# Cosine attention and leaky-ReLU MLP on one core: a written list of operations up to the third batch's second unit

## The chip, the cores and the metric

One core of a Trainium2 chip. The metric is device time in microseconds (us) of one execution. Engines are called as in the profile: PE is TensorE (PEld its weight loads), DVE VectorE, ACT ScalarE, POOL GpSimd, SP SyncE, which here only issues DMAs.

## The reference

```python
q_n = q / (norm(q) + 1e-06);  k_n = k / (norm(k) + 1e-06)
scores = q_n @ k_n^T / tau                       # tau = 0.1
attn = exp(scores - max);  attn = attn / (sum + 1e-09)
x = (attn @ v), heads side by side               # [3584, 768]
h = x @ w_in;  g = maximum(0.01 * h, h)          # w_in [768, 2048]
out = g @ w_out                                  # w_out [2048, 768]
```

8 batches, 12 heads, 448 positions, head size 64. Inputs are float32; the matmuls run in bf16.

## The kernel before, in words

**Slots.** The work on q and k is cut into 48 slots. In batches 0 and 1 a slot `s` is a pair of heads with q and k (slots 0 to 11, `OLD` = 12). From then on two slots make a unit: one holds q, the other k, of two pairs of heads. A slot goes through these steps:

- `load_qk` (L144): DMAs on SP into one of four `qk_h` buffers. Slots 0 to 5 come by `load_main` and `load_rem` (L129, L138) into `xT` memory.
- `squares` (L211): multiplies on POOL, for old slots in two parts (0 is q with the 64 remainder positions of q and k, 1 is the main part of k); slots 0 and 1 on ACT.
- `sums` (L228): reduce on DVE. `roots` (L244): Ln and Exp on ACT, which give the norms. `normalise` (L252): a small reduce, a reciprocal and one or two multiplies on DVE, which give `qn` in bf16.
- Old slots: `transposes` (L300), seven PE transposes into a PSUM bank and a DVE copy to `qkT`. New ones: a DVE transpose into `tt`, and after the unit's second slot six DMAs on SP from `tt` to `qkT`.

**Attention.** Old slots: `scores` (L334) makes a tile of scores of 128 keys for two heads (tile 3 holds the remainder keys of two slots), in two PSUM banks, and an ACT exp (L357) to a `pe` tile follows. For two slots together (`j`), `totals` (L375) adds up the exps on PE and takes Ln and inverse on ACT; `products` (L385) multiplies by v on PE, once for each parity `e` of the head size; `scale` (L394) writes to `xT` on DVE. New units: `quad_tiles` (L408) with exps at L425, then `group_products` (L429), `group_logs`, `group_inverse`, `group_scale`.

**MLP.** The tokens go in 8 chunks `c` of 384 and 512 columns in turn. `first(c, m)` (L487) is six matmuls against `w_in` and a Prelu on ACT into `hT`; with fewer `kts` it does part of the six, and the bank is kept. `second(c, ts, half)` (L525) is 16 matmuls against `w_out`, a DVE copy to `osb`, and an SP DMA to `out` when a row of results is full.

**Order.** `manual_schedule` (L48): each engine takes its instructions in the order in which the program names them, and semaphores hold what depends on another engine. For the first two batches the order is a loop over slots 0 to 5 (L654 to L736) and then a list of calls (L747 to L863). From there on a planner makes visits of three score tiles (L868 to L962): it deals the MLP's groups to visits by their cost, and gives each visit the steps of one slot.

**PSUM.** `banks` (L75) deals the eight banks: the one dealt longest ago. While `deals["apart"]` holds, which is until L747, pairs come out of banks 0 to 3 and single ones out of 4 to 7. An instruction that writes a bank waits until the earlier content has been read.

**Fills and holds.** `fill(n)` (L604) issues `n` matmuls on ones that nobody reads: 20 at the start (L611), 17 more among the first slots. `hold` (L617) is a copy of one element of `qn` on POOL: POOL's next work waits for that slot's `normalise`. It stands ahead of nearly all `squares`. `hold_loads` (L614) is an SP DMA of one element of `qn`: the next `load_qk` waits for it. It stands ahead of the loads of slots 8, 9, 12, 13 and 14.

**POOL's DMAs.** v (`load_v` L173, `load_v_rem` L180, `load_vq` L196), `w_in` in four pieces (L102) and `w_out` in three (L108) are issued on POOL, between the squares.

Of the kernel before, what the change touches and what calls it, by code (L numbers as in the profile page):

```python
# [12 lines left out]
AX = mybir.AxisListType  # L13


@with_exitstack
def kernel(
# [25 lines left out]
    WARM = 20  # L43
    NEWQ = 2 * NQ
    PER = 3
# [25 lines left out]
    age = [0] * 8  # L71
    kept = {}
    deals = {"n": 0, "apart": True, "width": 128}

    def banks(count, keep=None):  # L75
        lo, hi = (0, 8) if not deals["apart"] else (0, 4) if count == 2 else (4, 8)
        x = min(
            (i for i in range(lo, hi, count) if not set(range(i, i + count)) & set(kept.values())),
            key=lambda i: max(age[i : i + count]),
        )  # L80
        deals["n"] += 1
        age[x : x + count] = [deals["n"]] * count
        if keep:
            kept[keep] = x
        return ps[:, x] if count == 1 else ps[:, x : x + count]

    def given_back(keep):
        deals["n"] += 1
        age[kept.pop(keep)] = deals["n"]

# [115 lines left out]
    def squares(s, eng=gp, parts=(0, 1)):  # L211
        if s >= NSLOT:
            return
        sq = sqt[s % 3]
        if s >= OLD:
            sqs[s] = sq
            x = raw[s].rearrange("p (t d) -> p t d", d=D)
            gp.tensor_tensor(sq[:, :, :D], x, x, op=ALU.mult)  # L218
            return
        sqs[s] = halves(sq.rearrange("p t d -> p (t d)"), D + 1)  # L220
        for i in parts:
            x, y = raw[s][i], sqs[s][i]
            if eng is nc.scalar:
                nc.scalar.activation(y[..., :D], x, func=AF.Square)
            else:
                eng.tensor_tensor(y[..., :D], x, x, op=ALU.mult)  # L226

    def sums(s, parts=(0, 1)):  # L228
        if s >= NSLOT:
            return  # L230
        if s not in ss:
            ss[s] = smp.tile([128, 14], F32, name="ss")
        if s >= OLD:
            nc.vector.tensor_reduce(  # L234
                ss[s], sqs[s], axis=AX.X, op=ALU.add
            )
            return
        for i in parts:
            o = ss[s][:, 0:8] if i == 0 else ss[s][:, 8:14]
            nc.vector.tensor_reduce(  # L240
                o.rearrange("p (h t) -> p h t", h=2), sqs[s][i], axis=AX.X, op=ALU.add
            )

    def roots(s):  # L244
        if s >= NSLOT:
            return
        nc.scalar.activation(ss[s], ss[s], func=AF.Ln)  # L247
        nc.scalar.activation(norms[s % 3][:, :, 0], ss[s], func=AF.Exp, scale=0.5)  # L248
# [3 lines left out]
    def normalise(s):  # L252
        if s >= NSLOT:
            return
# [29 lines left out]
    def one(tp, s, lo, hi):  # L284
# [10 lines left out]
    def transposed():  # L295
        return banks(1).bitcast(BF16)[:, : 7 * 128].rearrange("p (t c) -> p t c", c=128)
# [3 lines left out]
    def transposes(s):  # L300
        if s >= NSLOT:
            return
        if s >= OLD:
            u, which = divmod(s - OLD, 2)
            if which == 0:
                turned[u] = ttp.tile([128, 2, 2, S], BF16, name="tt")
            to = turned[u][:, :, which].bitcast(F32)
            nc.vector.transpose(  # L308
                out=to.rearrange(("p g (c m) -> p m g c", "p g (m c) -> p m g c")[which], m=7),
                in_=qn[s].bitcast(F32).rearrange("p m (g c) e -> p m g (c e)", g=2),  # L310
            )
            if which == 0:
                return
            for w, pair in enumerate(UNITS[u][1]):
                dst = qtp.tile([128, 2, S], BF16, name="qkT")
                for r0, of, n, g in ((0, 0, 32, 0), (32, 0, 64, 1), (96, 32, 32, 0)):
                    nc.sync.dma_start(
                        out=dst[r0 : r0 + n],
                        in_=turned[u][64 * w + of : 64 * w + of + n, g],
                    )  # L320
                qkT[pair] = dst.rearrange("p t c -> p (t c)")
            return
        dst = qtp.tile([128, 7, 128], BF16, name="qkT")
        qkT[s] = dst.rearrange("p t c -> p (t c)")
        tp = transposed()
        one(tp, s, 0, 7)
        nc.vector.tensor_copy(out=dst, in_=tp)
# [6 lines left out]
    def scores(s, kis):  # L334
        key_tiles([(s, ki) for ki in kis])

    def key_tiles(which):

        tiles = []
        for s, ki in which:  # L340
            sc = banks(2)
            tiles.append(sc)
            width = deals["width"] if ki < 3 else min(deals["width"], 64)
            for p in range(0, 128, width):
                x, c0 = (qkT[s - 1 + p // 64], 448 + p % 64) if ki == 3 else (qkT[s], 512 + 128 * ki + p)
                for a in range(2):
                    rows = slice(64 * a, 64 * a + 64)
                    nc.tensor.matmul(  # L348
                        out=sc[p : p + width, a, :S], lhsT=x[rows, c0 : c0 + width],
                        rhs=x[rows, 0:S], start=True, stop=True,  # L350
                    )
        for (s, ki), sc in zip(which, tiles):
            if ki == 3:
                dst = pr[s // 2] = pe_tile()
            else:
                dst = pe[s, ki] = pe_tile()
            nc.scalar.activation(out=dst, in_=sc[:, :, :S], func=AF.Exp, scale=inv_tau)  # L357
# [17 lines left out]
    def totals(j):  # L375
        sm = banks(1)
        strip_products(j, sm, lambda g, ki: ones, lambda g: ones_rem[:, g // 2])
        rb = rbp.tile([128, 2, S], F32, name="rb")[:, 0]
        nc.scalar.activation(rb, sm[:, :S], func=AF.Ln)
        nc.scalar.activation(rb, rb, func=AF.Exp, scale=-1.0)  # L380
        rbs[j] = rb

    pos = {}

    def products(j, e, po=None):  # L385
        b, jj = divmod(j, NQ)
        if po is None:
            po = banks(1, (j, e))
        pos[j, e] = po
        vm = vb[j].rearrange("p h t (d e) -> p h t e d", e=2)  # L390
        vr = vrb[b % 2].rearrange("p j g (d e) -> p j g e d", e=2)
        strip_products(j, po, lambda g, ki: vm[:, g, ki, e], lambda g: vr[:, jj, g, e])

    def scale(j, e):  # L394
        b, jj = divmod(j, NQ)
        m, half = divmod(b, 2)
        if m not in xT:
            xT[m] = xtp.tile([128, KT, 2 * S], BF16, name="xT")
        nc.vector.tensor_tensor(
            xT[m][:, 2 * jj + e, half * S : (half + 1) * S], pos.pop((j, e))[:, :S], rbs[j],  # L400
            op=ALU.mult,
        )
        if (j, e) in kept:
            given_back((j, e))
# [3 lines left out]
    def quad_tiles(which):  # L408

        tiles = []  # L410
        for u, i in which:
            sc = banks(2)
            tiles.append(sc)
            for strip in range(4):
                x = qkT[UNITS[u][1][strip // 2]]
                c0 = S + 64 * i + 32 * (strip % 2)
                for a in range(2):
                    rows = slice(64 * a, 64 * a + 64)
                    nc.tensor.matmul(  # L419
                        out=sc[32 * strip : 32 * strip + 32, a, :S], lhsT=x[rows, c0 : c0 + 32],  # L420
                        rhs=x[rows, 0:S], start=True, stop=True,
                    )
        for (u, i), sc in zip(which, tiles):
            pq[u, i] = pe_tile()
            nc.scalar.activation(out=pq[u, i], in_=sc[:, :, :S], func=AF.Exp, scale=inv_tau)  # L425
# [3 lines left out]
    def group_products(g, e):  # L429


        us = [u for u, (gg, _) in enumerate(UNITS) if gg == g]
        two = len(us) == 2
        po = banks(2)
# [14 lines left out]
        return po  # L449

    def group_logs(g, po):
        grb[g] = rbp.tile([128, 2, S], F32, name="rb")
        nc.scalar.activation(grb[g], po[:, :, :S], func=AF.Ln)
# [10 lines left out]
    def group_scale(g, e, po):  # L464
        js = GROUPS[g]
        for w in range(2):
# [6 lines left out]
            for n in range(2):  # L473
# [4 lines left out]
                )  # L478

# [7 lines left out]
    def first(c, m, kts=range(KT)):  # L487
        c0, n = chunk_cols(c)
        if c not in hT:
            hT[c] = htp.tile([128, MT, 512], BF16, name="hT")  # L490
        if (c, m) in begun:
            pm, done = begun.pop((c, m))
        else:
            pm, done = banks(1, (c, m, "begun") if len(kts) < KT else None), 0
# [7 lines left out]
        if done + len(kts) < KT:  # L502
            begun[c, m] = pm, done + len(kts)
            return
        if (c, m, "begun") in kept:
            given_back((c, m, "begun"))
        nc.scalar.activation(out=hT[c][:, m, :n], in_=pm[:, :n], func=AF.Prelu, alpha=0.01)  # L507

# [16 lines left out]
    def second(c, ts, half):  # L525
# [472 lines left out]
```

## Time and profile before

| | |
|---|---|
| time, 3 runs | 415.45, 415.52, 416.83 us; median 415.52 |
| the profiled execution | 416.8 us; its span in the trace 415.0 us |
| PE busy | 405.8 us, 98% of the span |
| ACT, DVE, POOL busy | 250.5 (60%), 221.4 (53%), 115.1 (28%) us |
| chain that ended last | PE 93%, DMA 2%, ACT, POOL, SP queue and issue 1% each |
| DMA | 53.8 MB, 130 GB/s over the span |

The span runs from the first instruction to the end of the last; 1.8 us of the profiled time lie around it. Busy time of an engine counts time in which it has an instruction under way. PE's matmuls overlap, so that a busy PE need not be one at its best pace. The chain is followed back from the last instruction: at each step to what released it, or to the instruction ahead of it on its engine. "Idle before" in a row of the timeline is the time that the engine stood still ahead of it, and what ended it.

### The profile page before, as it was taken

To read this page: it belongs to the slowest core of one execution; us is meant where nothing else is said; L and a number is where in the kernel's file an instruction comes from. 1 tells how busy PE (TensorE), PEld (TensorE's weight loads), DVE (VectorE), ACT (ScalarE), POOL (GpSimd) and SP (SyncE) were. 2 spreads that over 40 slices of the span, in tenths; PEclk is the share of its full clock that TensorE was granted. 3 is DMA by queue.
4 is the path that set the end of the run, shared out by engine and by line. 5 is a ranking of instruction groups with operands and counts; after the bars stand their busy time and mean duration, and the time that the engine had idled before them with its cause. 6 is when DMAs were issued, how large, how long until landed. Compare 5 with 4: busy or idle time off the path is not lost.

```text
span 415.0 us, 11326 instructions
## 1 busy us (share of the span) xinstructions
PE 405.8 (98%) x4783; PEld 212.2 (51%) x4799; DVE 221.4 (53%) x387; ACT 250.5 (60%) x431; POOL 115.1 (28%) x150
## 2 busy tenths in 40 slices
PE   8799999999999999999999999999999999999997
PEld 3235555544555555544455555554445555654465
DVE  5878879756778556766484964464621301210021
ACT  4997877378657785667865688547764464004300
POOL 4885556133234132413331433122210000000000
PEclk9999999999999999999999999999999999999999
DMA  7999998965377851884285681742442100020022
GB/s 184 233 208 222 216 232 176 258 178 127 57 208 184 206 127 24 206 230 97 51 190 153 149 235 44 173 128 84 91 90 66 53 39 3 38 77 0 2 76 76
DMA packets 41980, 53.82 MB, mean 130 GB/s; under 512 B 12490, under 2 KB 32330, under 8 KB 41930
## 3 DMA queue, kind: packets, MB, share of 16 engines
q1 hardware_dynamic: 25738, 41.01, 35.1%
q0 software_dynamic: 15504, 11.80, 19.8%
q8 instruction: 37, 0.61, 0.6%
q10 hardware_dynamic: 688, 0.30, 0.2%
q14 instruction: 13, 0.11, 0.1%
HBM read 45.61 MB, written 11.01 MB: 136 GB/s over the span
## 4 chain that ended last, share of the span: by engine, by line
PE 93%; DMA 2%; ACT 1%; POOL 1%; SPq 1%; issue 1%; DVE 0%; POOLq 0%
PE ps L533 36%; PE ps L496 36%; PE ps L444 9%; PE ps L419 7%; PE ps L368 3%; PE ps L348 2%; DMA xT<-in_k_dram 1%; DMA xT<-in_q_dram 1%; ACT pe L357 1%; POOL sq L226 1%; PE ps L286 1%; SPq L133 0%; DVE qn L272 0%; POOL v_rem L186 0%; SPq L141 0%
## 5 line engine op out<-in xcount | busy, mean ns | idle before, releaser
L533 PE MATMUL ps<-w_out_sb,hT 128*128 128x384 bf16 (+1 forms) x912 | 151.3, 323 | 0.0
L496 PE MATMUL ps<-xT,w_in_sb 128*128 128x384 bf16 (+1 forms) x754 | 150.1, 352 | 0.8 <-issue 0.2
L425 ACT ACTIVATE pe<-ps 128x896 bf16<-128x896 f32 x126 | 108.9, 916 | 47.1 <-PE ps L419 47.1
L533 PEld LDWEIGHTS <-hT 128*128 128x128 bf16 x912 | 86.5, 98 | 64.0 <-issue 10.3
L496 PEld LDWEIGHTS <-w_in_sb 128*128 128x128 bf16 x768 | 72.6, 98 | 74.3 <-issue 9.8
L507 ACT ACTIVATE hT<-ps 128x384 bf16<-128x384 f32 (+1 forms) x128 | 67.4, 553 | 56.1 <-PE ps L496 54.9
L543 DVE COPY osb<-ps 128x384 f32<-128x384 f32 (+1 forms) x57 | 31.2, 547 | 101.4 <-PE ps L533 101.3
L218 POOL TENSOR_TENSOR sq<-qk_h 128x896 f32<-128x896 f32 x36 | 60.9, 1691 | 13.0 <-DMA qk_h<-in_k_dram 8.5
L618 POOL CAST seen<-qn 128x1 f32<-128x1 bf16 x46 | 8.5, 185 | 166.3 <-DVE qn L262 156.5
L262 DVE TENSOR_TENSOR qn<-qk_h,r 128x896 bf16<-128x896 f32 x36 | 43.3, 1203 | 1.2
L234 DVE TENSOR_REDUCE ss<-sq 128x14 f32<-128x910 f32 x36 | 37.9, 1053 | 1.1 <-POOL sq L218 1.1
L357 ACT ACTIVATE pe<-ps 128x896 bf16<-128x896 f32 x42 | 36.0, 918 | 2.4 <-PE ps L348 2.3
L419 PE MATMUL ps<-qkT 64*32 64x448 bf16 x1008 | 36.5, 353 | 0.0
L255 DVE TENSOR_REDUCE r<-norms 128x14 f32<-128x28 f32 x48 | 8.6, 178 | 48.7 <-ACT norms L248 48.1
L469 DVE TENSOR_TENSOR xT<-ps,rb 128x448 bf16<-128x448 f32 x32 | 18.4, 615 | 23.2 <-PE ps L444 21.5
L308 DVE STREAM_TRANSPOSE tt<-qn 128x448 f32<-128x448 f32 x36 | 29.6, 821 | 0.9
L444 PE MATMUL ps<-pe,vq 64*32 64x448 bf16 x1008 | 27.0, 349 | 0.0
L247 ACT ACTIVATE ss<-ss 128x14 f32<-128x14 f32 x48 | 10.3, 215 | 23.6 <-DVE ss L234 23.1
L419 PEld LDWEIGHTS <-qkT 64*32 64x32 bf16 x1008 | 13.0, 91 | 19.2 <-issue 14.2
L444 PEld LDWEIGHTS <-vq 64*32 64x32 bf16 x1008 | 14.5, 92 | 8.0 <-issue 0.3
L444 PE MATMUL ps<-pe,ones 64*32 64x448 bf16 x560 | 15.1, 349 | 0.0
L348 PE MATMUL ps<-qkT 64*64 64x448 bf16 (+1 forms) x132 | 12.8, 359 | 2.1 <-ACT pe L357 1.2
(53 smaller groups left out, 218.1 us busy)
## 6 DMA issues: line engine op xcount, KB each, us to landing
qk_h<-in_q_dram SPq DMA_DIRECT2D x36, 224.0 KB, 4.1
qk_h<-in_k_dram SPq DMA_DIRECT2D x36, 224.0 KB, 4.6
out_dram<-osb SPq DMA_DIRECT2D x20, 384.0 KB, 2.3
qkT<-tt SPq DMA_DIRECT2D x72, 56.0 KB, 3.2
qkT<-tt SPq DMA_DIRECT2D x36, 112.0 KB, 3.4
vq<-in_v_dram POOLq DMA_DIRECT2D x16, 224.0 KB, 4.7
w_in_sb<-in_moe_w_in_dram POOLq DMA_DIRECT2D x4, 768.0 KB, 10.4
out_dram<-osb SPq DMA_DIRECT2D x15, 192.0 KB, 3.7
```

Of the source, the lines that this page charges most:

```text
L218: gp.tensor_tensor(sq[:, :, :D], x, x, op=ALU.mult)
L234: nc.vector.tensor_reduce(ss[s], sqs[s], axis=AX.X, op=ALU.add)
L262: nc.vector.tensor_tensor(qn[s].rearrange("p m d e -> p m e d"), raw[s].rearrange(f"p ({t[1:-1]} d) -> p m e d", e=n, d=D), r.rearrange(f" ...
L308: nc.vector.transpose(out=to.rearrange(("p g (c m) -> p m g c", "p g (m c) -> p m g c")[which], m=7), in_=qn[s].bitcast(F32).rearrange("p ...
L357: nc.scalar.activation(out=dst, in_=sc[:, :, :S], func=AF.Exp, scale=inv_tau)
L419: nc.tensor.matmul(out=sc[32 * strip : 32 * strip + 32, a, :S], lhsT=x[rows, c0 : c0 + 32], rhs=x[rows, 0:S], start=True, stop=True,)
L425: nc.scalar.activation(out=pq[u, i], in_=sc[:, :, :S], func=AF.Exp, scale=inv_tau)
L444: nc.tensor.matmul(out=po[32 * strip : 32 * strip + 32, w, :S], lhsT=weights, rhs=pq[us[x if two else 0], i][rows, a, :], start=(i == 0), ...
L496: nc.tensor.matmul(out=pm[:, :n], lhsT=w_in_sb[:, kt, m * 128 : (m + 1) * 128], rhs=xT[c // 2][:, kt, c0 : c0 + n], start=(done + i == 0), ...
L507: nc.scalar.activation(out=hT[c][:, m, :n], in_=pm[:, :n], func=AF.Prelu, alpha=0.01)
L533: nc.tensor.matmul(out=po2[:, : hi - lo], lhsT=hT[c][:, m, ts * 128 : (ts + 1) * 128], rhs=w_out_sb[:, m, half * HALF + lo : half * HALF + ...
L543: nc.vector.tensor_copy(out=o[:, cols], in_=po2[:, : hi - lo])
```

## The change

The loops, the list of calls and the planner go. In their place stands one string, `ORDER`, with 1221 steps, and a table that gives each name its function. A step is a name and whole numbers: `sq.2.1` squares of slot 2, part 1; `su` sums, `ro` roots, `no` normalise, `tp` the PE transposes and `tc` their copy, `tt` and `td` the DVE transpose and its DMAs, `k` and `x` a tile of scores and its exp, `q` and `y` the same of new units, `to`, `ln`, `in` totals with Ln and inverse, `pr` and `sc` products and scale, `g`, `gl`, `gi`, `gx` the same of groups, `f` and `r` first and its Prelu, `s` and `o` second and its copy and DMA, `w` fills, `lq`, `lv`, `lr`, `wi`, `wo`, `lg` loads, `hp` and `hr` holds, `tg` the end of the split of PSUM banks. Matmuls and what reads them are now separate steps.

```diff
+ORDER = """
+sq.2.1 w.2 lq.6 w.20 w.2 w.2 qf.0.0.3 sq.2.0 qf.1.0.3 uf.0.0.3 qf.0.3.4 uf.1.0.3 uf.0.3.4 ro.0 no.0 sa.1.1
+sa.1.0 su.1.0 tg lv.0 w.2 w.2 tp.0.0.4 tp.0.4.7 lr.0.0.2 ta.0.0.4 su.1.1 tc.0.4.7 sq.3.1 k.0.1 k.0.0 ro.1
+su.2.1 sq.3.0 no.1 k.0.2 hr lr.0.2.4 tp.1 w.2 x.0.0 x.0.2 x.0.1 wi.0 sq.4.1 su.2.0 tc.1 k.1.3 k.1.2 lv.1 ro.2
+x.1.3 x.1.2 k.1.0 su.3.1 lq.7 no.2 sq.4.0 x.1.0 su.3.0 tp.2 k.1.1 ro.3 tc.2 k.2.2 x.1.1 k.2.1 lq.8 x.2.2 x.2.1
+k.2.0 to.0 no.3 su.4.1 sq.5.0 tp.3 tc.3 sq.5.1 w.2 pr.0.1 wi.1 x.2.0 hp.2 k.3.0 su.4.0 ln.0 k.3.1 su.5.0 ro.4
+w.2 pr.0.0 x.3.0 no.4 k.3.2 sq.7.1 k.3.3 x.3.1 in.0 x.3.2 tp.4 su.5.1 tc.4 sc.0.0 w.3 sq.6.1 lv.2 ro.5 wi.2
+k.4.2 x.3.3 k.4.0 no.5 sq.6.0 to.1 lq.9 pr.1.0 sc.0.1 x.4.0 tp.5 ln.1 k.4.1 tc.5 pr.1.1 in.1 wi.3 sq.7.0 x.4.2
+sc.1.0 sc.1.1 su.6.1 su.6.0 sq.8.1 sq.8.0 hp.5 x.4.1 k.5.0 k.5.1 su.7.0 su.7.1 su.8.1 f.0.0.0.2 f.0.1.0.2
+x.5.0 x.5.1 k.5.3 wo.0 lv.4 sq.9.1 k.5.2 f.0.0.1 f.0.1.1 f.0.1.3 f.0.0.3 su.8.0 sq.9.0 x.5.3 x.5.2
+f.0.3.0.1.2.3 f.0.2.0.1.2.3 ro.6 to.2 ro.7 ln.2 in.2 no.6 pr.2.1 pr.2.0 sc.2.1 tp.6 sc.2.0 f.0.5 f.0.3.4.5
+r.0.3 f.0.0.4.5 f.0.1.4.5 su.9.1 tc.6 no.7 r.0.0 r.0.1 ro.8 f.0.4 lq.10 k.6.0 su.9.0 no.8 k.6.2 r.0.4 lq.11
...
+k.8.0 sq.11.0 k.8.1 k.9.2 to.3 no.10 x.8.0 x.9.2 ln.3 f.0.13 f.0.6 tp.10 r.0.13 x.8.1 r.0.6 k.9.0 tc.10
+su.11.1 su.13 lq.12 su.11.0 k.9.1 k.9.3 s.0.0.0.384 sq.12 x.9.3 k.8.2 x.9.1 x.9.0 ro.11 k.10.2 k.10.1 no.11
...
+"""
-    WARM = 20
...
-    def banks(count, keep=None):
+    def take(name, count):
         lo, hi = (0, 8) if not deals["apart"] else (0, 4) if count == 2 else (4, 8)
+        busy = {b for x, n in taken.values() for b in range(x, x + n)}
...
+    def give(name):
+        x, count = taken.pop(name)
         deals["n"] += 1
         age[x : x + count] = [deals["n"]] * count
...
+    for step in ORDER.split():
+        name, *args = step.split(".")
+        steps[name](*map(int, args))
```

What differs in the order, engine by engine (counted by writing out the old order in the same names):

- **PE.** The first 148 steps differ, up to unit 2's third score tile; from there the order is the same. Ahead of slot 0's transposes stand 30 fills (20 before), behind them 9 (17 before). Within a slot the tiles of scores come in another order (`k.1.3` first, for one), and the `first` groups of chunks 0 and 1 in another.
- **ACT, DVE.** The first 132 and 98 steps differ, the same work in another order. DVE does slot 3's `normalise` ahead of all sums of slot 4, where it stood behind the first of them. ACT does slot 1's `roots` ahead of slot 0's exps, as before.
- **POOL.** 25 of 46 holds on `qn` are gone: those on slots 0, 1, 3, 4, 6, 8, 10 to 18, 21, 26, 31 to 34, 36, 40, 42 and 47. Holds on slots 2 and 5 remain in the head. `load_v` of slots 8 and 9 (`lv.4`) comes ahead of that of slots 6 and 7 (`lv.3`). This part reaches beyond the third batch: behind it the other engines' order is as it was, and POOL has fewer holds.
- **SP.** All five `hold_loads` are gone. Slot 13 is loaded ahead of 12, 18 ahead of 16 and 17.
- **PSUM.** A bank is dealt by when it was last given back by its reader, where it was by when it was dealt; a bank that is still to be read is not dealt. The split into pairs and single banks ends ahead of slot 0's transposes, where it ended behind slot 5's scores.

## The prediction

> **What bounds the kernel now.** I read the page first (busy shares, slices), then the chain of waits in order of time, then busy times by stage, then the timeline of the first 40 us. Busy times by stage, columns in the order PE, PEld, DVE, ACT, POOL, clock, DMA share, GB/s:
>
> ```profile
> 10.00:20.00 10.00, 7.36 (x62) 2.77 (x62) 8.34 (x18) 9.06 (x16) 8.03 (x12) 1.00 1.12 240
> 20.00:26.90 6.90, 6.04 (x69) 2.43 (x72) 6.48 (x15) 6.01 (x11) 5.90 (x10) 1.00 1.15 192
> 26.90:37.00 10.10, 9.80 (x133) 4.48 (x132) 7.78 (x16) 8.32 (x15) 9.02 (x13) 1.00 1.17 226
> 37.00:108.00 71.00, 70.79 (x756) 36.18 (x766) 49.98 (x85) 52.50 (x98) 27.47 (x33) 1.00 0.91 188
> 108.00:412.00 304.00, 303.37 (x3750) 163.06 (x3744) 142.45 (x231) 169.89 (x283) 60.63 (x74) 1.00 0.42 107
> ```
>
> From 37 us on TensorE is busy 374.2 of 375 us, and the chain has nothing but PE pieces from 30.45 to 412.11. I checked that this busy time is work and not hidden waiting: from slot 6's transposes at 37.07 I added up the matmuls in the written order (0.1625 us per 384 columns, 2.60 for 16 of them; 0.216 per 512 columns; 0.19 per score tile; 0.75 per products pass; 0.39 per transposes; 0.11 at each change of tile shape). The sum puts the first `second` at 55.59 (trace 55.68) and visit 0's first scores at 81.06 (trace 81.24). So behind 37 us there is nothing to win, and only the order can lose something. Before 37 us it is the head that counts:
>
> ```profile
> 1.66 7.34 PE L607 MATMUL ps<-pe 128*128 128x512 bf16 x20 [1.66 <-DVE pe L590]
> ...
> 6.72 1.16 DVE L272 TENSOR_TENSOR qn<-xT,r 128x512 bf16<-128x512 f32 x2
> ...
> 6.75 0.15 PEld L607 LDWEIGHTS <-pe 128*128 128x128 bf16 x1 [0.28 <-issue]
> ...
> 7.17 0.15 PEld L607 LDWEIGHTS <-pe 128*128 128x128 bf16 x1 [0.28 <-issue]
> ...
> 7.54 0.96 PEld L607 LDWEIGHTS <-pe 128*128 128x128 bf16 x5 [0.21 <-issue]
> ...
> 8.83 0.55 PE L286 MATMUL ps<-id,qn 128*128 128x128 bf16 x7
> ...
> 9.22 0.81 PE L607 MATMUL ps<-pe 128*128 128x512 bf16 x3
> ...
> 10.37 2.54 ACT L357 ACTIVATE pe<-ps 128x896 bf16<-128x896 f32 x3 [0.17 <-PE ps L348]
> ...
> 13.11 2.27 POOL L226 TENSOR_TENSOR sq<-xT 128x512 f32<-128x512 f32 x2 [0.91 <-DMA xT<-in_k_dram]
> ...
> 13.97 1.82 DVE L272 TENSOR_TENSOR qn<-xT,r 128x512 bf16<-128x512 f32 x2
> ...
> 19.71 1.16 DVE L272 TENSOR_TENSOR qn<-xT,r 128x512 bf16<-128x512 f32 x2
> ...
> 26.88 0.75 PE L368 MATMUL ps<-pe,ones 128*32 128x448 bf16 x12
> ```
>
> Three things are to be seen. The fills stand 0.43 us apart until about 7.5 (weight loads at 6.75, 7.17), then (0.81 - 0.38) / 2 = 0.215. The first transposes start at 8.83, when the 20 fills end, though `qn` was there at 7.88. And ACT is 9 of 10 us busy from the first exp at 10.37.
>
> **The change, part by part.**
>
> *Fills.* Before: 20, then 17 in small lots behind the first transposes. After: 2+20+2+2+2+2 = 30 ahead of them, 9 behind. Ten more at 0.215 put the first transposes at 8.83 + 2.15 = 10.98. The copy to `qkT` follows by 0.42 and takes 0.59, slot 1's `roots` (0.50) stand behind it on ACT: the first exp moves from 10.37 to 12.5. This is the one sure loss, 2.1 us, and PE, ACT and DVE all inherit it.
>
> *ACT to the end of slot 3's exps.* Same work in both orders up to the exp of the remainder keys of slot 3: 14 exps, four `roots`, one Ln and one inverse. Before it ran from 10.37 to 26.5 with idle marks of 0.50, 0.64, 0.17 and 0.08: 16.1 - 1.4 = 14.7 of work. After, scores are no longer confined to four banks (`together` comes ahead of the first transposes), slot 1's remainder tile goes first, and `normalise` no longer queues behind `sums` of a later slot (before, DVE waited 1.22 us for POOL's squares of slot 4 ahead of slot 3's `normalise`). I walked the first slots by hand: `normalise` of slot 1 ends about 14.2, its copy 15.5, so ACT still waits about 0.4 at slot 1's first exp and 0.3 further on. 12.5 + 14.7 + 0.7 = 27.9. Of 2.1 us, 0.7 is won back.
>
> *PE from `totals(1)` to slot 6's transposes.* The same set of matmuls in both. Before it took from 26.88 to 37.07, 10.2 us, some 0.5 of it waits. `totals` may start a little ahead of the last exp (its last four matmuls alone need it): 27.7. Its bank is that of the first `scale`, done about 27.3, so that does not hold it. 27.7 + 10.2 = 37.9. Against 37.07: **+0.85 us**. Between the ends: all waits gone and no ACT idle, 27.0 + 9.7 = 36.7, or -0.4; DVE contention as below, +2.9.
>
> *Holds.* 25 of 46 one-element copies on POOL go (0.185 us each, 4.6 us in all, on an engine that is idle 72%: worth nothing). What they kept apart is POOL's squares and DVE's `normalise`. The two meet at 13.11 to 15.79: the multiply took 1.82 in place of 1.16, the squares 2.27 in place of 1.82. At 67.53 one took 2.16 in place of 1.17, beside a square from 66.96 to 68.64. So a meeting costs DVE 0.66 to 1.0. The Trainium skill says the same in general (GPSIMD Engine Reference, 8. Key points): GpSimd shares its SBUF interfaces with VectorE, and contends with instructions of two SBUF inputs, which `normalise` is; the rule speaks against this change, and the trace agrees. Behind 130 us it costs nothing: `qn` is due some four visits ahead, 20 us, cover enough for 1 us. In the head slots 1 to 5 are exposed; at 0.66 each the range gets up to 3.3, if every one lands on the path. I take 0.2 for it, since ACT has exps of the slot before to go on with.
>
> *`hold_loads`.* Five SP DMAs go (0.65 us each on the queue, hidden). Slots 8 and 9 are now asked for at about 17.6 instead of 21.7 and 26.4, as soon as older loads land. That puts some 0.5 MB ahead of `w_in`'s second piece (issued 20.1, landed 30.1). The stage rows have 192 to 240 GB/s from 10 to 37 us, so 0.5 MB is some 2.5 us: landed about 32.6, needed at 33.7. Cost nothing, with 1.1 us of cover; without it a stall of the same size. `w_out`'s first half landed at 52.9, needed at 56.6: 0.46 MB more ahead of it is about 2 us, still covered.
>
> *Behind 37 us.* I redid the running sum in the new order: the same total, 57 changes of shape in place of 66 over the differing part, of which 30 in place of 31 behind slot 6's transposes, and both orders meet at unit 2's scores (108.3). Banks: I listed for each matmul group the last reader of its bank. The closest are 1.1 to 1.3 us behind (before: 0.81, without a visible stall), one of them the first `second`, whose bank waits for a Prelu that queues behind an exp: 0.4 us. I take **+0.3**; bounds 0 and 2.
>
> *Sum.* +0.85 + 0.2 + 0.3, rounded down for the shapes saved ahead of 37 us: **+1.2 us**. Against the profiled execution (span 415.0, 416.8 with what lies around it) that is 418.0. That execution stood at the upper end of the runs shown; against their median of 415.52 it is **416.7**.
>
> **The rivals.**
>
> *Head recovered in full.* If four score pairs keep ACT without idle time and PE without waits, slot 6's transposes come at 36.7 and the rest costs nothing: 415.1 to 415.8. For it: the banks; against it: DVE's chain for slot 1 starts 2.1 late as well.
>
> *Contention in the chain (slower).* Place: `normalise` of slots 1 to 5. Price 0.66 to 1.0 each; it decides from the point where a slot's copy to `qkT` ends later than the exp before it, and by my walk slots 1, 2 and 3 stand within 0.5 us of that. Three hits: +1.2 + 2.2 = +3.4, so 418.9. Speaking for it is the row at 13.97.
>
> *Late fills run slow again (slower).* PE's small lots of fills behind the first transposes shrink from 17 to 9, so it idles more between 12 and 24 us. If it fell back to the pace of the first 7.5 us once, work that takes 2.9 us would take 5.9: +2.9, so 419.6. The granted clock shows 1.00 through all gaps of before, up to 1.35 us. The Trainium skill (TensorE: Matmul & The Clock Gate, Part 1: The HAM clock gate) has such a fall after an idle window, and warm-up as a matter of time, not of matmul count; the first half no run here shows, the second fits the fills.
>
> *The ten fills cost nothing.* If all fills ran 0.215 apart, 30 would end at 8.1, ACT would start as before and gain its 1.4 idle, the DVE order its share: -2.5, so 413.0. Against it: the rows at 6.75 and 7.17.
>
> **How the numbers follow.** Forecast (416.0 to 417.6) 0.45; head recovered 0.22; contention 0.23; slow again 0.06; fills free 0.04. About 0.5%, 2.1 us, is what a measurement of this kernel can tell from no change: 413.4 to 417.6 counts as the same. Faster 0.04; same 0.45 * 0.85 + 0.22 = 0.60; slower 0.07 + 0.23 + 0.06 = 0.36. The range leaves out the fills' gain and the far end of the slow cases: 414.8 to 419.8.
>
> **What would show it.** Right: 30 fills end near 11.0, first exp at 12.4 to 12.6, ACT idle under 1 us to slot 3's last exp, slot 6's transposes at 37.5 to 38.5, PE without waits of over 0.5 us behind that. Wrong: transposes of slot 6 ahead of 37.0; a PE wait for `w_in_sb` near 33 or for `w_out_sb` near 56; `normalise` rows of 1.8 us and more in slots 1 to 5 with PE waiting for `qkT` behind each; PE gaps between 40 and 108 us.

## The result, and the profile after

| | before | after |
|---|---|---|
| first comparison, median (lowest to highest) | 416.25 (415.45 to 416.83) us, 6 runs | 422.00 (419.49 to 425.65) us, 6 runs |
| ratio, 95% interval | | 1.0147 (1.0109 to 1.0185): slower by 1.5% |
| repeated later | 416.16 us, 17 runs | 424.42 us, 6 runs; 1.0159 (1.0122 to 1.0196) |

Ratio and interval are worked out over the single executions, so that they need not be the quotient of the medians; those of the repeat leave out one execution, of 426.15 us, as in the slow state.

The forecast was 416.7 with a range to 419.8; the time is 422.0. The kernel before took 415.2 to 418.1 us in all its executions but one (420.1); the changed one comes in two groups: of its 15 executions here, 5 took 419.5 to 420.4 us and 10 took 422.3 to 426.2. The profile of the first comparison is of a short one (419.49 us, span 417.7), so I read that first and the long ones below (e15, e17).

The chain of the page, after (before: PE 93%, DVE 0%):

```profile
PE 91%; DVE 4%; DMA 2%; POOL 1%; SPq 1%; issue 1%; DVEq 0%
```

Busy times by stage, after, columns as before (PE, PEld, DVE, ACT, POOL, clock, DMA share, GB/s):

```profile
10.00:20.00 10.00, 4.89 (x41) 2.10 (x42) 9.25 (x17) 7.22 (x14) 9.94 (x14) 0.95 1.16 229
20.00:30.00 10.00, 9.33 (x104) 3.46 (x105) 9.35 (x17) 8.48 (x15) 9.94 (x13) 0.88 1.15 226
30.00:37.00 7.00, 6.53 (x75) 3.00 (x63) 7.00 (x12) 6.42 (x10) 4.75 (x6) 1.00 1.20 209
37.00:108.00 71.00, 70.73 (x788) 36.59 (x790) 50.83 (x89) 51.50 (x102) 26.41 (x23) 1.00 0.89 181
108.00:415.00 307.00, 305.83 (x3761) 164.05 (x3769) 145.41 (x234) 172.26 (x287) 60.13 (x64) 1.00 0.43 107
```

From 10 to 20 us GpSimd is busy 9.94 of 10 (before 8.03), VectorE 9.25 (8.34), TensorE 4.89 (7.36). TensorE is nearly full again from 37 us on. The head in the timeline, after:

```profile
1.66 8.49 PE L666 MATMUL ps<-pe 128*128 128x512 bf16 x30 [1.66 <-DVE pe L650]
9.99 0.55 PE L372 MATMUL ps<-id,qn 128*128 128x128 bf16 x7
11.64 1.73 ACT L436 ACTIVATE pe<-ps 128x896 bf16<-128x896 f32 x2 [0.28 <-PE ps L425]
11.88 2.00 DVE L357 TENSOR_TENSOR qn<-xT,r 128x512 bf16<-128x512 f32 x2
15.89 2.65 DVE L357 TENSOR_TENSOR qn<-xT,r 128x512 bf16<-128x512 f32 x2
20.15 2.23 DVE L357 TENSOR_TENSOR qn<-xT,r 128x512 bf16<-128x512 f32 x2
25.48 2.10 DVE L357 TENSOR_TENSOR qn<-xT,r 128x512 bf16<-128x512 f32 x2
29.69 2.10 DVE L357 TENSOR_TENSOR qn<-xT,r 128x512 bf16<-128x512 f32 x2
```

These five rows are `normalise` of slots 1 to 5, a pair of multiplies each. Before, four took 1.16 to 1.19 and one 1.82. And TensorE stands behind them; its waits up to 30 us (total, times, longest; before 1.3, once):

```profile
PE ps L372 <- DVE qn L357: 4.4, 5, 1.3
```

Slot 6's transposes begin at 39.61 (before 37.07), and the last matmul ends at 414.46 (412.07). From the one to the other it is 374.85 us, before 375.0: the short execution loses all of its 2.4 us in the head.

### The profile page after: what moved, and what is told of

Its sections match the earlier page's. It is cut to its first block, busy times and chain, and to the rows that moved or that the text cites. A ratio compares the mean times of both kernels' runs of the same rounds, so it can differ in the third digit from the quotient of the medians.

```text
span 417.7 us, 11279 instructions
## 1 busy us (share of the span) xinstructions
PE 405.7 (97%) x4784; PEld 212.6 (51%) x4799; DVE 227.5 (54%) x387; ACT 249.9 (60%) x431; POOL 113.2 (27%) x125
## 4 chain that ended last, share of the span: by engine, by line
PE 91%; DVE 4%; DMA 2%; POOL 1%; SPq 1%; issue 1%; DVEq 0%
PE ps L602 36%; PE ps L566 35%; PE ps L516 9%; PE ps L490 7%; PE ps L448 3%; DVE qn L357 2%; DMA xT<-in_q_dram 2%; PE ps L425 2%; DVE ss L317 1%; POOL sq L304 1%; PE ps L372 1%; SPq L209 0%; DVE qkT L388 0%; SPq L217 0%; POOL w_in_sb L180 0%
## 5 line engine op out<-in xcount | busy, mean ns | idle before, releaser
L347 DVE TENSOR_TENSOR qn<-qk_h,r 128x896 bf16<-128x896 f32 x36 | 44.8, 1245 | 1.3
L675 POOL CAST seen<-qn 128x1 f32<-128x1 bf16 x21 | 3.9, 183 | 121.6 <-DVE qn L347 120.4
L304 POOL TENSOR_TENSOR sq<-qk_h 128x384 f32<-128x384 f32 (+1 forms) x12 | 11.8, 999 | 12.3 <-DMA qk_h<-in_k_dram 12.0
```

The costliest lines, as they stand in the source:

```text
L347: nc.vector.tensor_tensor(qn[s].rearrange("p m d e -> p m e d"), raw[s].rearrange(f"p ({t[1:-1]} d) -> p m e d", e=n, d=D), r.rearrange(f" ...
```

## The experiments

The theory after this reading: GpSimd's squares, no longer held, stretch VectorE's multiplies in the head (1), and ten more fills ahead delay everything (2). The rivals: TensorE falls back to half clock (the trace has it from 19.08 to 22.49 us) and that is the loss; or the order itself, its visits, costs the time. Each kernel is compared with the kernel before on the same chip.

| kernel | median us | ratio (95%) |
|---|---|---|
| e1 after, GpSimd's head as before | 418.95 | 1.0058 (1.0039 to 1.0076) |
| e2 after, 20 fills ahead | 419.50 | 1.0077 (1.0062 to 1.0092) |
| e3 after, 16 more fills in the waits | 423.47 | 1.0183 (1.0152 to 1.0214) |
| e4 before, without the holds on slots 0, 1, 3, 4 | 419.46 | 1.0077 (1.0053 to 1.0101) |
| e5, e16 after, hold on slot 10 | 420.78, 421.36 | 1.0115 (1.0090 to 1.0141), 1.0105 (1.0076 to 1.0134) |
| e6 = e1 + e2 + e5 | 417.82 | 1.0040 (1.0024 to 1.0055) |
| e7 = e6 + two load holds | 417.75 | 1.0034 (1.0022 to 1.0045) |
| e8 before, 30 fills ahead | 417.32 | 1.0025 (1.0014 to 1.0036) |
| e9 = e7 + ten fills in the waits | 418.27 | 1.0032 (1.0021 to 1.0044) |
| e10 before, ten fills moved ahead | 417.77 | 1.0013 (1.0003 to 1.0023) |
| e11 = e5 + all fills as before | 419.25 | 1.0057 (1.0045 to 1.0069) |
| e12 = e9 + sums moved behind | 416.45 | 0.9999 (0.9989 to 1.0009) |

**e1, GpSimd's head as before.** The steps of GpSimd alone, in order; the other engines' order stays.

```diff
-sq.2.1 sq.2.0 lv.0 lr.0.0.2 sq.3.1 sq.3.0 hr lr.0.2.4 wi.0 sq.4.1 lv.1 sq.4.0 sq.5.0 sq.5.1 wi.1 hp.2 sq.7.1
-sq.6.1 lv.2 wi.2 sq.6.0 wi.3 sq.7.0 sq.8.1 sq.8.0 hp.5 wo.0
+hr lr.0.0.2 hp.0 sq.2.0 sq.2.1 lv.0 hp.1 sq.3.0 sq.3.1 lr.0.2.4 wi.0 hp.2 sq.4.0 sq.4.1 lv.1 wi.1 hp.3
+sq.5.0 sq.5.1 lv.2 hp.4 sq.6.0 sq.6.1 wi.2 hp.5 sq.7.0 sq.7.1 wi.3 wo.0 sq.8.0 sq.8.1
```

> The changed kernel, with POOL's order up to the squares of slot 8 as it was before, holds on slots 0, 1, 3 and 4 included; every other engine's order as changed. Theory 'squares beside normalise': the multiplies of normalise in slots 1 to 5 fall back from 2.0 to 2.65 us to about 1.2, the granted clock stays at 1.00, slot 6's transposes start at or ahead of 38, and the time is 415.5 to 417.5. Rival 'order and fills' (the 30 fills ahead and the new order of PE, ACT and DVE make the loss): still 419 to 424, with normalise short but slot 6's transposes late.

418.07 to 419.33 us, no long execution in four. `normalise` of slots 1 to 5 takes 1.16, but for 1.49 at slot 3; slot 6's transposes begin at 38.95, not at or ahead of 38. So the squares beside `normalise` are a cause: without these meetings the long executions are gone, and against the short ones (median of five 419.75) 0.8 us is won. But the expected 417.5 is missed: 0.58%, 2.4 us, stays.

**e2, 20 fills ahead in the changed order.**

```diff
-sq.2.1 w.2 lq.6 w.20 w.2 w.2
+sq.2.1 w.2 lq.6 w.10 w.2 w.2
```

> The changed kernel with 20 instead of 30 fills ahead of the first transposes. If the late start is what counts, the time falls by up to 2.1 us, to about 420, and slot 6's transposes come as much earlier. If squares beside normalise set the pace, the start is earlier by 1 to 2 us but the time stays within 1 us of 422, since POOL's squares and the multiplies still meet; fewer fills may even bring the half clock on earlier.

First transposes at 8.43, first exp at 10.35; slots 1 to 5 still take 1.79 to 2.77, and slot 6's transposes come at 39.10. No long execution in four either. The first transposes are 1.56 us earlier and slot 6's only 0.5: most of the earlier start is lost again on the way, and the fall from 422.0 to 419.5 is mainly that of the long executions.

**e3, more fills while TensorE waits.**

```diff
-tp.1 ... tp.2 ... tp.4 ... tp.5
+w.4 tp.1 ... w.6 tp.2 ... w.3 tp.4 ... w.3 tp.5
```

> The changed kernel with 16 more fills put where PE waits for normalise: 4, 6, 3 and 3 ahead of the transposes of slots 1, 2, 4 and 5. Theory 'half clock': PE no longer idles long enough, the granted clock is 1.00 in every run, the time falls to 418 to 419.5 and hardly scatters (the changed kernel went from 419.5 to 425.7, with clocks of 0.996 to 0.984). Rival 'squares beside normalise alone': clock up, but the time stays at 421 to 422, as the chain runs through DVE.

The clock stays full to 63.98 us, and the time grows to 423.47. So a full clock in the head does not bring the time back. Sixteen fills take time too (slot 6's transposes begin at 40.58, 0.97 later than without them), so the price of the half clock itself is left to e7 and e9. This trace showed a second place: slot 10's multiplies at 56.20 took 6.30 us beside three squares, though slots 1 and 2 took 2.01 and 2.64 here as in the short executions; in the kernel before, a hold on slot 10 keeps the next squares behind them.

**e4, the kernel before without four holds.**

```diff
-    hold(qn[0][:, 6, 0, 0:1])
     squares(2)
...
-        else:
+        elif s in (1, 4):
             hold(qn[s + 1][:, 6, 0, 0:1])
```

> The kernel before, without the holds on slots 0, 1, 3 and 4 (the four that the change takes out of the head); nothing else is changed. Theory 'squares beside normalise': multiplies of 1.8 us and more in several of slots 1 to 5, and 1.5 to 5 us more, 418 to 421. Rival: the holds are worth nothing here by themselves, 415.5 to 417.

With nothing else changed, 0.8% slower: slots 3 and 4 take 2.69 and 2.10, slot 6's transposes begin at 38.91 in place of 37.07. The times stand in pairs, 418.6 twice and 420.3 twice.

**e5 and e16, the hold on slot 10 given back** (the same kernel twice).

```diff
-ro.10 sq.13 r.0.8 k.8.0 sq.11.0 k.8.1 k.9.2 to.3 no.10 x.8.0
+ro.10 r.0.8 k.8.0 k.8.1 k.9.2 to.3 no.10 hp.10 sq.13 sq.11.0 x.8.0
```

> The changed order with one hold of GpSimd given back: the squares of the slots behind slot 10 wait for its normalise, as they do in the kernel before. The theory is that the missing hold lets GpSimd run squares back to back beside slot 10's two multiplies, that these then take from 2.64 us (profiled execution of the changed kernel) to 6.30 us (the kernel with more fills), and that TensorE waits for them in the middle and falls to half clock: this is the scatter from 419.5 to 425.7. By it the time lies at 419 to 420.5 with less scatter, and slot 10's multiplies take about 1.2 us. The rival is that the scatter comes from the head alone: then the time stays about 422 and scatters by 3 us or more.

> The changed order with the hold on slot 10 given back, once more, for the number of its long executions. With the first four it took 420.42 to 421.81 us. The theory is that without the meeting at slot 10 no execution takes over 422.5 us; the rival is that the long ones come from elsewhere and show here in half of the executions too.

Eleven executions, 419.33 to 421.91: none longer, where ten of 15 of the changed kernel are. Slot 10's multiplies take 1.16 in both profiles. The expected 419 to 420.5 us is missed all the same (420.78 and 421.36).

**e14, e15, e17 and e13: the changed kernel again, for a long execution in a profile.**

> The changed kernel as it is, for more executions and another profile: it scattered from 419.49 to 425.65 us, and only its fastest was profiled. The theory is that the slower executions lose their time behind slot 10's multiplies, where nothing holds GpSimd, with TensorE's clock at half afterwards: the times come in two groups, about 420 and about 424 to 425.5, the lower granted clock with the longer time, and if the profiled one is long, slot 10's multiplies take 4 us or more there. The rival is that the long ones lose it in the head: then slot 6's transposes begin later than at 41 us in a long one and slot 10's multiplies take under 3 us.

> The changed kernel once more, for a profile of one of its longer executions (about 424 us, six of the twelve so far). The theory is that a long one shows slot 10's multiplies at 4 us or more and a half clock between 50 and 70 us; the rival is that it shows the head longer, with slot 6's transposes behind 41 us.

> The same as the look before it, in case that one falls on a short execution.

> The same as the two looks before it, in case both fall on short executions.

e13's profile and e14 are short (419.75, 419.62), e15 and e17 long (424.74, 424.13). The timeline of e15, POOL and DVE:

```profile
11.74 3.11 DVE L357 TENSOR_TENSOR qn<-xT,r 128x512 bf16<-128x512 f32 x2
12.60 1.83 POOL L304 TENSOR_TENSOR sq<-xT 128x384 f32<-128x384 f32 x2
16.86 3.41 DVE L357 TENSOR_TENSOR qn<-xT,r 128x512 bf16<-128x512 f32 x2
...
56.39 1.69 POOL L298 TENSOR_TENSOR sq<-qk_h 128x896 f32<-128x896 f32 x1
56.67 4.91 DVE L357 TENSOR_TENSOR qn<-qk_h,r 128x512 bf16<-128x512 f32 x2
58.03 1.50 POOL L304 TENSOR_TENSOR sq<-qk_h 128x512 f32<-128x512 f32 x1
59.50 1.67 POOL L298 TENSOR_TENSOR sq<-qk_h 128x896 f32<-128x896 f32 x1
```

Its chain:

```profile
56.67 4.92 DVE qn L357 x2
...
62.68 4.39 PE ps L602 x16
```

and slot 10 in the short e13:

```profile
55.47 1.16 DVE L357 TENSOR_TENSOR qn<-qk_h,r 128x512 bf16<-128x512 f32 x2
```

In the two other short profiles slot 10 took 2.64 and 2.65, and its transposes began 18.26 us behind slot 6's as in e13: the place has cover for that much.

A long execution differs in two places. In the head slots 1 and 2 take 3.11 and 3.41 (e17: 2.76 and 3.42) in place of 2.00 and 2.65, and slot 6's transposes begin at 40.77 (41.82), not at 39.6 to 39.9. And at slot 10 the squares of slots 13, 11 and 12 are back to back just when the multiplies want to start: 4.91 (4.92). In e15 TensorE then has half clock from 63.18 for 3.41 us, and the first 16 matmuls of `second` take 4.39, not 2.71. From slot 6's transposes to the last matmul it is 378.9 (377.2) us, against 374.85 in the short ones: 4.1 and 2.4 us behind the head. Of this, 2.4 us is in both the wait of slot 10's last three transposes for the second multiply; the other 1.7 of e15 is the 16 matmuls at half clock. e16's profile (419.33 us) has the short head (slots 1, 2: 2.00, 2.64), e5's (421.81) the long one (3.13, 3.42): with the hold on slot 10, a long head costs its 2.4 us and no more. Both my theory of slot 10 and its rival, the head, hold in part: in e15 and e17 the long head comes first, and slot 10 adds to it; e3 shows that slot 10 can be long behind a short head. The heads differ in a race of GpSimd and VectorE. Of the eight profiles with 30 fills ahead and no holds on slots 0, 1, 3 and 4, five have a short head (the first one, e3, e13, e14, e16): there slot 1's second multiply begins 0.07 to 0.14 us ahead of GpSimd's first square of slot 3 (12.49 and 12.59 in the first one). In the three with a long head (e5, e15, e17) it begins 0.01 to 1.32 us behind it (12.61 and 12.60 in e15). No run changed this alone, so it is an observation, not a cause shown.

**e6 and e7, the causes given back together.** e6 has the edits of e1, e2 and e5; e7 also:

```diff
+no.3 hs.3 lq.8
...
+no.4 hs.4 lq.9
```

> The changed order with three things of the kernel before: GpSimd's order and holds in the head, the hold on slot 10, and 20 fills ahead instead of 30. If these three are the causes, the time is within 1 us of the kernel before, 415.5 to 417.2, slot 6's transposes begin at about 37.1 us and every normalise of slots 0 to 5 takes about 1.2 us. The rival is that the other moves of the order (visits, loads, evictions) cost time of their own: then it stays at 418 or more.

> The kernel with the three things given back, and the two holds ahead of the issue of the later loads as well, with the issues where the kernel before has them. The theory prices these two holds at nothing: within 1 us of the kernel without them. The rival is that loads issued early slow the multiplies or the loads needed first: then it is faster by 1 us or more.

Most of the loss goes, and the load holds are worth nothing; but both miss 417.2 us, and the rival's 418 is as near; slot 6's transposes begin at 38.68 in e6 and 37.05 in e7 (37.1 expected). Half clock is granted for 6.83 us in each, so I tried that next, together with the price of the fills.

**e8, e9, e10, e11: the fills.** e8 has 30 ahead in the kernel before, e10 takes ten of the others away as well:

```diff
-    WARM = 20
+    WARM = 30
...
-    fill(3)
...
-        elif not last:
+        elif s == 3:
             fill(2)
...
-            fill(2)
+            if s == 3:
+                fill(2)
             if s == 3:
...
-            fill(2)
+            fill(s if s == 1 else 2)
```

e9 (on e7) and e11 (on e5, with `w.20` as `w.10`) put ten fills into the waits:

```diff
+w.3 k.0.1 ... w.2 k.0.2 ... w.2 k.1.2 ... w.2 tp.2 ... w.1 k.2.2
```

> The kernel before with 30 fills ahead instead of 20 and nothing else changed. The theory is that ten more fills put off the first transposes by about 2.1 us and that most of it stays: 417.8 to 418.8 us. The rival is that the wait for the first transposes' input or the faster clock makes up for it: then it is 416.0 to 416.6.

> The kernel with four things given back (GpSimd's head, the hold on slot 10, 20 fills ahead, the two load holds), and as a fifth the other ten fills where the kernel before has them: three behind the transposes of slot 0, two ahead of each of three steps of the first two slots, one later. With the ten fills missing there, TensorE's clock was granted at half for 6.83 us in this kernel's relative without them. The theory is that those fills kept TensorE busy enough while it waited, and that the half clock is what is left of the loss: 415.8 to 416.9 us, no half clock between 8 and 60 us. The rival is that the other moves of the order cost the remaining 1.5 us: then it stays at 417.3 to 418.3 though the clock is full.

> The kernel before with nothing changed but ten fills, which stand ahead of the first transposes (30 there) instead of in the waits of the first two slots. The same kernel with 30 ahead and all of its other fills took 417.32 us. The theory is that the missing ones let the clock fall to half for 3.4 to 6.8 us, and that this costs another 0.5 to 2 us: 417.8 to 419.3. The rival is that fills in the waits do nothing, or stand in the way: then it is 416.5 to 417.3.

> The changed order with the hold on slot 10 and all fills where the kernel before has them, but without the holds of the first slots. The same with the fills as changed took 420.78 us. The theory is that the squares beside the multiplies of the first slots cost some 3 us by themselves, clock or no clock: 418.3 to 420. The rival is that the doubled multiplies cost only by the half clock that they bring, and that the fills keep it full: then it is 416 to 417.5.

e8: ten more fills ahead cost 1.0 us (first transposes at 10.04), under the 1.5 expected and over the rival's 0.3. e10, against the kernel before, is no slower than e8. Its times come in two groups, five of 416.65 to 417.07 us and seven of 417.77 to 417.89. The profile, of the first group, shows no half clock in the head, but eight of the twelve executions have a mean clock of 0.996, six of them in the second group; so whether the fills in the waits matter in that order is open. e9 and e7 compare the clock; their stage rows:

```profile
10.00:20.00 10.00, 7.76 (x65) 2.74 (x61) 8.32 (x19) 8.04 (x13) 8.18 (x13) 1.00 1.15 246
```

```profile
10.00:20.00 10.00, 6.49 (x46) 2.20 (x46) 8.15 (x18) 8.01 (x14) 8.18 (x13) 0.71 1.12 237
```

Granted clock 0.71 in e7, 1.00 in e9 (the weight loads of e9's fills take 0.10 us all through the waits; at half clock they take 0.15), and the ratio is 1.0034 and 1.0032. From slot 0's transposes to the end of slot 6's it is 29.7 and 29.4 us. So my clock theory falls: while TensorE waits for other engines, its slower matmuls cost 0.3 us there and nothing in the time, provided that the ten fills that e9 also has cost nothing. e11 says the same within one kernel: three executions with a mean clock of 0.996 took 419.18 to 419.45 us, three with 1.00 took 419.12 to 419.93. e11 itself came as its theory had it (418.3 to 420): with all fills back, GpSimd's head still costs. Against e9 it gives GpSimd's order and holds in the head, with the two load holds: 0.0025, 1.0 us.

**e12, VectorE's sums moved.** What e9 still loses stands in its waits of TensorE from 30 to 120 us (total, times, longest):

```profile
PE ps L424 <- DVE qkT L387: 1.0, 1, 1.0
PE ps L371 <- DVE qn L356: 0.8, 1, 0.8
```

and in its chain:

```profile
40.91 1.22 POOL sq L303
...
43.85 0.55 DVE qn L356
44.40 0.54 DVE qkT L387
```

VectorE takes its steps in the written order. The new list puts `su.9.0` ahead of slot 8's `normalise` and slot 7's copy, and GpSimd's square for it ends at 42.12; so the copy that TensorE wants waits for a sum that nobody needs yet. In the kernel before, both sums of slot 9 stand behind that copy. In the changed kernel itself these sums hold up nobody: without `hold_loads` slot 9's data lands at 33.47 (40.75 in e9) and its squares end at 36.41, and behind 30 us TensorE waits 0.4 us in all for VectorE.

```diff
-su.8.0 ... no.6 ... su.9.1 tc.6 no.7 r.0.0 ... su.9.0 no.8 ... tc.7 f.0.10
+no.6 su.8.0 ... tc.6 no.7 su.9.1 r.0.0 ... no.8 ... tc.7 su.9.0 f.0.10
```

> The kernel with five things given back, which took 418.27 us (418.3 against 416.9 of the kernel before, 1.0032 of it), and three steps of VectorE moved in the written order: the sums of slot 8's second half go behind slot 6's normalise, those of slot 9 behind slot 7's normalise and copy. In its profile VectorE stands at these sums until GpSimd's squares are done, and TensorE then waits 1.0 us for slot 7's copy and 0.8 us for a normalise. The theory is that these two waits are what is left of the loss: a ratio of 0.999 to 1.0015, some 416.4 to 417.5 us, and no wait of TensorE for VectorE over 0.4 us between 30 and 60 us. The rival is that the time behind slot 6 is lost elsewhere: then it stays at 1.0025 to 1.004 though the waits are gone.

Ratio 0.9999, and no wait for `qn` or `qkT` is left between 30 and 120 us. A wait of 0.7 for `xT`, which VectorE writes, is new, against the expected 0.4, and 0.3 for `w_in`. By the ratio the rival, a loss elsewhere, falls. Where the gain lies the profile does not show: it is of the slowest of the twelve executions (417.29 us), and from the end of slot 6's transposes to the last matmul it has 375.6 us, as e9 has (375.7; 374.5 before). With six things given back the new order is as fast as the old one, and not faster.

## Why the prediction was wrong, point by point

- **The fills: the pace right, the price by luck.** Forecast 10.98 for the first transposes and 12.5 for the first exp; 9.99 and 11.64 came, because TensorE's full clock began at 5.42 us there and at 7.45 in the profile before. Over the runs it began between 4.51 and 7.45; 20 fills end at 7.5 to 8.8 us, 30 at 9.8 to 10.7. The net price of 0.85 measured 1.0 (e8), but in the old order: what was to win part of it back, ACT's smoother run in the new order, did not come. The fills behind the first transposes were 19 before, not 17: the program has 19, and the trace has 39 weight loads of fills before and after, while two rows of matmuls are missing. So ten fills moved ahead and none went.
- **ACT to slot 3's last exp: wrong.** Forecast 27.9 with 0.7 won back on the way; it ended at 29.34, so 1.5 was lost on the way. My hand walk used 1.16 for each `normalise`; slots 1 to 3 took 2.00, 2.65 and 2.23.
- **The holds in the head, 0.2 us: the step that failed.** I named the mechanism, priced it at 0.66 to 1.0 for each meeting, and then took almost nothing, since ACT has exps to go on with. They did not cover it: up to 30 us TensorE waits 4.4 us for `qn` where it waited 1.3, and the sign that I had set for this, rows of 1.8 us and more with PE waiting behind them, is there at all five slots. In the short executions all five slots met squares, not one to three, at 0.84 to 1.49 us each; in the long ones two did, at 1.60 to 2.26. GpSimd without holds is busy 9.94 of 10 us, so few multiplies miss it. Alone, on the kernel before, the four holds are worth 0.8% (e4); in the changed order, with fills and slot 10's hold given back, 1.0 us together with GpSimd's order and the load holds (e11 against e9).
- **Behind 37 us, +0.3 with bounds 0 and 2: wrong in the long executions.** In the short ones nothing was lost there (374.85 against 375.0 us). "Behind 130 us it costs nothing" stands: no wait of TensorE for VectorE is left there. But between 37 and 130 us I priced PE's shapes and banks and not the holds: slot 10's is the one that decides (2.4 and 4.1 us in the long executions). And I did not look at which sums stand ahead of which `normalise` on VectorE in slots 6 to 9. That cost nothing in the changed kernel, where the squares come early; with the holds given back slot 8's squares end at 35.5 (e6) and not at 30.8, slot 9's data comes late (e9), and the new order of the sums stands in the way: 1.4 us (e9 to e12, 0.0033).
- **`hold_loads`, nothing: right** (e6 to e7). `w_in`'s second piece landed at 32.5 (forecast 32.6), by luck: it was asked for 1.8 us later than before, at 21.92, and took 10.6 us in place of 10.0.
- **The rivals.** "Contention in the chain", chance 0.23, 418.9 us, was the case that came; its place, slots 1 to 5, was right and its price too low, and it lacked slot 10. "Late fills run slow again", 0.06: the fall came (half clock from 19.08 us for 3.41), at 0.3 us or less in the head (e7 and e9); where TensorE is the bound it costs, as 4.39 for 2.71 in e15. That part of the Trainium skill (TensorE: Matmul & The Clock Gate, Part 1: The HAM clock gate), which no run had shown before, is now seen, with a difference: its table speaks of an idle window, and here TensorE was busy for 20 to 58% of the step of 3.41 us ahead of each fall.

**The sum as the runs have it.** By place, a short execution loses its time in the head: slot 6's transposes come 2.5 us late, behind `normalise` rows of twice the length. By what was given back, its 419.75 - 416.3 = 3.4 us go in three steps: to 2.4 with the fills and the hold on slot 10 (e11), to 1.3 with GpSimd's head and the load holds (e9), to nothing with the sums (e12). The last step is no part of the changed kernel's own loss, as its sums held up nobody; so these steps do not price its causes one by one. The parts are not independent: e4 has 3.2 for holds that are worth 1.0 in the changed order, and e1 and e2 each also take the long executions away. Long executions add 1.2 to 2.2 us in the head and 2.4 to 4.1 at slot 10. That the squares beside the multiplies cost is shown (e1, e4, e5); how the 3.4 us divide among squares, fills and order is not.

## What to carry to other kernels

A wait on an engine that is idle 72% of the time may be what keeps it from another engine's way: before a hold goes, look at what it separates, multiply the price of a meeting by the number of slots that will meet, and walk the chain with the longer durations. Check the in-order engines for reductions that stand ahead of a copy or a multiply that somebody waits for. And profile more than one execution when the spread grows from 1 to 6 us: the one profiled may be of the short kind.

## What the runs showed of the hardware that was not expected

- **Multiplies and squares do not share, they take turns.** In e15 the two multiplies of slot 10, 0.69 and 0.55 us alone (e13), took 1.97 and 3.02; the first ended 0.56 after the first square did, the second began during the second square, let the third go first as well, and ended 0.42 after it. The Trainium skill (SBUF — State Buffer, SBUF: two separate sides) calls it an exclusive lock for a whole instruction, held by whichever starts first. The trace agrees (squares 1.69, 1.50 and 1.67 against 1.67, 1.03 and 1.67 in e13; multiplies 2.8 to 5.5 times as long), and adds that a waiting multiply can lose to a second square behind the first. The recorded starts do not always tell who holds the lock: in the short head slot 1's second multiply, at 12.49, began 0.10 us ahead of a square and still took 1.39, while the square took its 0.84. GpSimd's DMA issues alone mostly do not do this: the first multiply at 11.88 took 0.69 beside one. But in e2 slot 1's second multiply, at 11.29, took 1.18 in place of 0.55 beside three issues and no square, and in the short executions slot 2's first took 1.33, though its first square beside it began 1.05 us after it did. Why is open.
- **The clock falls after half-busy windows.** It changes in steps of 3.41 us, whose phase differs from run to run, so that the same kernel shows 0.984 to 0.996. In the head its stretches last 3.41, 6.83, 10.24, 13.65 or (e4) 17.07 us. Added up from the matmul rows, TensorE had been busy 20 to 58% of the step ahead of a fall; steps of 58 and 63% passed without one in the kernel before, and one of 55% in e11, from 23.39 us. Where exactly it decides is open.
